# Two expert layers on one core: the low parts of a weight matrix in pieces of 1024 and 768 columns instead of 512 and 384

## The chip, the core and the metric

The kernel runs on one core of one Trainium2 chip. The metric is the device time of one execution in microseconds (us); the median of several runs is compared. TensorE multiplies matrices into the PSUM banks, VectorE and ScalarE work element by element, GpSimd does gathers, scatters and small arithmetic, and SyncE issues most transfers. Each engine works through its own queue in order and waits for others by semaphores.

## What is computed

The input is 14336 rows of 192 numbers. A causal convolution of 7 taps, one set of taps for each of 8 heads, comes first; the taps are a softmax. Then two layers of 8 experts follow, each expert with weights `w1` (192 x 1024) and `w2` (1024 x 192). Cut to what matters:

```python
x = conv(x, softmax(weight))
keep = x @ w_skip > 0                       # first layer: only these rows
e = argmax(x @ w_gate); g = softmax(...)[e]
x[keep] += g * (relu(x @ w1[e]) @ w2[e])
e = argmax(x @ w_gate2 + bias[modality])    # second layer: all rows
out = g * (relu(x @ w1[e]) @ w2[e])
```

## The kernel before

Products are made in half precision, with each number split into a high and a low part: high is the number, scaled by a power of two, rounded to 16 bits; low is the rounded rest. A product then takes three or five matmuls in place of one. So every weight matrix has to be *prepared* before it is used: loaded as 32-bit numbers, its power of two found, its high part rounded by ScalarE, and its low part formed by VectorE.

The work goes in three stages, which overlap. The first (to about 178 us) makes the convolution and the gate scores for 128 tiles of 112 rows, in 8 groups of 16 tiles, and the tables that say which row goes to which expert. The second (about 136 to 475 us) takes the first layer in blocks of 128 rows that belong to one expert. The third takes the second layer, mostly in pairs of blocks.

A block of the second stage is: 40 matmuls of 128 columns with `w1b` (the prepared `w1`) into two PSUM halves; for each half ScalarE writes `hh`, the high part after the relu, and VectorE `hlo`, the low part; and 24 matmuls of 192 columns with `w2b` on `hh` and `hlo` of the block before. VectorE then adds the residual into `x2a` or `x2s`. Two PSUM banks, later three, take turns for the halves, so TensorE can run a half or two ahead of `hlo`, not more.

The preparations are written as a generator, `prep`. It is run in two lanes beside the blocks: lane 0 prepares the eight experts of the first layer right into the buffers `w1b` and `w2b` that the blocks read, and lane 1 prepares four experts of the second layer into the buffers `o1` and `o2` (in the trace both are `o`). Both also store the result to memory (`s1a`, `s2a`, `s1b`, `s2b`; function `keep`, lines 409 and 411). Twelve preparations run in all; four more stand in a loop at the end that is entered only where the routing needs it.

What sets the order: `yield p` hands control back, and `prep` goes on `p` ticks later. There are four ticks in a block; p is 8 beside the blocks of the second stage (two blocks), 14 in the first stage, and 8 in lane 1. On TensorE, VectorE, ScalarE and GpSimd the instructions stand in the order in which the program writes them. On SyncE the compiler's scheduler places them.

One preparation, lines 368 to 392: `wt` holds the first 128 rows of `w1`, `wr` its other 64 rows (loaded in two transfers of 64 partitions), `w2t` all of `w2`. They lie in the buffers `ws1` (three slots) and `ws2` (one slot), both `ws` in the trace. The scales are in `sc` (`wsc` in the trace). Every low part is one VectorE instruction of the same form,

```python
nc.vector.scalar_tensor_tensor(out, v, scale, high, ALU.mult, ALU.subtract)
```

so it reads the 32-bit weights and the high part, both in SBUF, and writes 16 bits. The loads of the next expert are issued in between: `loadt` (line 308), `loadr` (line 315) once `wt` has been read, and `load2` (line 320) once `w2t` has been read.

Nearly all instructions of the trace carry line 71, that of the helper that records them; they are told apart by the names of their tiles.

Of the kernel before, what the change touches and what calls it, by code (L numbers as in the profile page):

```python
# [11 lines left out]
AF = mybir.ActivationFunctionType  # L12
ALU = mybir.AluOpType
# [4 lines left out]
D = 192  # L18
E = 8
F = 1024  # L20
# [95 lines left out]
class Moe:  # L116
# [179 lines left out]
    def prep(self, ws, pool, pq, dst, guard, done, es, lane, lag, pace, free, busy, first, early, side):  # L296
        nc = self.nc
        g = self.gram[lane].rearrange("p (i c) -> p i c", i=2)
        sq = g[:, 0, 0:2]

        def which(k, e):
            if k == 0:
                return slice(e, e + 1)
            return bass.ds(nc.sync.value_load(self.sel[0:1, e:e + 1], min_val=0, max_val=7), 1)

        def loadt(k, e):
            wt = pool.tile([128, F], F32, name="ws1", bufs=3)
            nc.sync.dma_start(wt, ws[k][0][which(k, e), 0:128, :].rearrange("a p f -> (a p) f"))
            return wt

        def loadr(k, e):
            wr = pool.tile([128, F], F32, name="ws1", bufs=3)
            x = which(k, e)
            for hf in range(2):
                nc.sync.dma_start(wr[hf * 64:hf * 64 + 64, :], ws[k][0][x, 128:192, :].rearrange("a p f -> (a p) f"))
            return wr

        def load2(k, e):
            w2t = pool.tile([128, 8 * D], F32, name="ws2", bufs=1)
            nc.sync.dma_start(w2t, ws[k][1][which(k, e)].rearrange("a p f -> (a p) f"))  # L320
            return w2t

        nxt = (loadt(*es[0]), loadr(*es[0])), load2(*es[0])
        yield first
        for n, (q, e) in enumerate(es):
            (wt, wr), w2t = nxt
            if early() and n < 2:
                for i, vs in enumerate(((wt,) * 8 + (wr[0:64],) * 8, (w2t,) * 12)):
                    for k, v in enumerate(vs):
                        c = k % 8 if i == 0 else k  # L330
                        v = v.bitcast(BF16)[:, c * 256 + 1:c * 256 + 256:2]
                        nc.tensor.matmul(g[:, i, :], v, v, start=(k == 0), stop=(k == len(vs) - 1))
                    yield 1
                yield 2
                dg = pq.tile([128, 512], F32, name="dg", bufs=1)[:, 0:256].rearrange("p (i c) -> p i c", i=2)
                nc.vector.tensor_tensor(dg, g, self.identf.unsqueeze(1).to_broadcast([128, 2, 128]), ALU.mult)
                ssq = pq.tile([128, 2], F32, name="ssq")
                nc.vector.tensor_reduce(ssq, dg, AX.X, ALU.add)
                yield 3
                nc.tensor.matmul(sq, self.ones, ssq, start=True, stop=True)  # L340
            else:
                sa = pq.tile([128, 4], F32, name="sa", bufs=2)
                for k, v in ((0, wt), (2, wr), (1, w2t[:, 0:4 * D]), (3, w2t[:, 4 * D:])):
                    jk = pq.tile([128, 512], F32, name="dg", bufs=1).bitcast(BF16)[:, 0:v.shape[1]]
                    nc.scalar.activation(jk, v, AF.Square, accum_out=sa[:, k:k + 1])
                    yield 2 if k < 3 else 5
                nc.tensor.matmul(sq, self.ones, sa[:, 0:2], start=True, stop=False)
                nc.tensor.matmul(sq, self.ones, sa[:, 2:4], start=False, stop=True)
            yield 2
            sc = pq.tile([128, 2], F32, name="wsc")  # L350
            self.pow2(sq, sc)
            nc.vector.tensor_scalar(sc, sc, 2.0 ** 30, 2.0 ** FT, ALU.min, ALU.mult)
            yield 1 if early() else 3
            while not guard(q, e) or busy[0]:
                yield 1
            busy[0] = True
            o1, o2 = dst(q, e)
            o2v = o2[:, :W2C].rearrange("p (c j) -> p c j", c=8)
            w2v = w2t.rearrange("p (c j) -> p c j", c=8)
            kf = pq.tile([128, 1], F32, name="kf")  # L360
            nc.vector.scalar_tensor_tensor(kf, sc[:, 0:1], 2.0, sc[:, 1:2], ALU.mult, ALU.mult)
            nc.vector.tensor_scalar(o2[:, W2C:].bitcast(I32), kf.bitcast(I32), EXPM, EXPM, ALU.bitwise_and, ALU.bitwise_xor)
            last = n + 1 == len(es)
            p = pace()
            if not last:
                nwt = loadt(*es[n + 1])
            h = F // 2
            lo = lambda o, v, s, i: nc.vector.scalar_tensor_tensor(o, v, s, i, ALU.mult, ALU.subtract)
            nc.scalar.activation(o1[:, 0, :], wt, AF.Copy, scale=sc[:, 0:1])
            yield p  # L370
            nc.scalar.activation(o2v[:, 0:4, 0:D], w2v[:, 0:4], AF.Copy, scale=sc[:, 1:2])
            lo(o1[:, 1, 0:h], wt[:, 0:h], sc[:, 0:1], o1[:, 0, 0:h])
            yield p
            lo(o1[:, 1, h:], wt[:, h:], sc[:, 0:1], o1[:, 0, h:])
            yield p
            nc.scalar.activation(o2v[:, 4:8, 0:D], w2v[:, 4:8], AF.Copy, scale=sc[:, 1:2])
            lo(o2v[:, 0:2, D:], w2v[:, 0:2], sc[:, 1:2], o2v[:, 0:2, 0:D])
            yield p
            lo(o2v[:, 2:4, D:], w2v[:, 2:4], sc[:, 1:2], o2v[:, 2:4, 0:D])
            if not last:  # L380
                nxt = (nwt, loadr(*es[n + 1]))
            yield p
            lo(o2v[:, 4:6, D:], w2v[:, 4:6], sc[:, 1:2], o2v[:, 4:6, 0:D])
            yield p
            nc.scalar.activation(o1[:, 2, :], wr, AF.Copy, scale=sc[:, 0:1])
            nc.vector.scalar_tensor_tensor(o2v[:, 6:8, D:], w2v[:, 6:8], sc[:, 1:2], o2v[:, 6:8, 0:D], ALU.mult, ALU.subtract)
            yield p
            nc.vector.scalar_tensor_tensor(o1[:, 3, 0:F // 2], wr[:, 0:F // 2], sc[:, 0:1], o1[:, 2, 0:F // 2], ALU.mult, ALU.subtract)
            if not last:
                nxt = nxt, load2(*es[n + 1])  # L390
            yield p
            nc.vector.scalar_tensor_tensor(o1[:, 3, F // 2:], wr[:, F // 2:], sc[:, 0:1], o1[:, 2, F // 2:], ALU.mult, ALU.subtract)
            done[q].add(e)
            busy[0] = False
            st = self.keep(ws, q, e, o1, o2, free)
            if early():
                for w in st:
                    yield w
                if not last:
                    yield max(1, lag() - 3 * (2 + q))  # L400
            else:
                side.add(st)
                if not last:
                    yield 4 + 12 * q
# [1178 lines left out]
```

## Time and profile before

| | before |
|---|---|
| median of three runs | 1002.71 us (1000.71 to 1004.94) |
| the profiled execution | 1001.22 us |
| its span, first to last instruction | 999.3 us |
| TensorE busy | 916.0 us (92%) |
| VectorE busy | 587.8 us (59%) |
| GpSimd busy | 513.7 us (51%) |
| ScalarE busy | 476.0 us (48%) |
| low parts of weights on VectorE | 96 instructions, 67.4 us together |

Times in the trace count from the span's start. "PE" is TensorE, "DVE" VectorE, "ACT" ScalarE, "POOL" GpSimd and "SP" SyncE. A duration in the trace runs from an instruction's start to its end, and consecutive VectorE instructions overlap a little, so the time that one takes from the queue is read from start to start. A busy TensorE is not TensorE at its peak: matmuls that follow one another more slowly still count as busy, so the number of matmuls in a stretch is read beside it.

### The profile page before, as it was taken

What the parts mean: (1) busy time and instruction counts of PE and PEld (TensorE: products, weight loads), DVE (VectorE), ACT (ScalarE), POOL (GpSimd) and SP (SyncE); (2) the same over time, 40 slices, a digit from 0 to 9 for tenths busy, and PEclk for the clock granted to TensorE, in tenths of its full rate; (3) what the DMA queues carried; (4) which work ended last, traced back from release to release, by engine and by line L of the source; (5) the groups of instructions that cost most, each with busy time, mean ns of one, the idle gap of its engine ahead of it and who ended that gap; (6) DMA issues with size and microseconds to landing.
All of it is one profiled execution on the core that took longest, in us unless ns stands there. A gap on an engine that the chain in (4) does not pass through costs nothing. (4 is left out here: it accounts for less than half of the span.)

```text
span 999.3 us, 28865 instructions
## 1 busy us (share of the span) xinstructions
PE 916.0 (92%) x11000; PEld 852.3 (85%) x11000; DVE 587.8 (59%) x1624; ACT 476.0 (48%) x895; POOL 513.7 (51%) x985
## 2 busy tenths in 40 slices
PE   6999868997999999976999999999989999999993
PEld 4666668987999999976888988999988999999992
DVE  5689977899798877543555465864332333333330
ACT  3877743545686654443645654333333333333430
POOL 4155543742646365562777675454544555555431
PEclk9999859999999999997999999999999999999997
DMA  9595576754868776599333333222492222332240
GB/s 318 192 334 187 186 198 191 197 137 132 237 181 249 214 223 197 163 233 329 91 95 98 109 98 111 70 64 62 135 295 63 73 74 69 74 73 74 74 122 16
DMA packets 106197, 150.79 MB, mean 151 GB/s; under 512 B 80591, under 2 KB 85689, under 8 KB 100800
## 3 DMA queue, kind: packets, MB, share of 16 engines
q1 hardware_dynamic: 91424, 119.34, 38.6%
q0 software_dynamic: 13920, 28.87, 12.1%
q8 instruction: 89, 1.46, 0.6%
q10 hardware_dynamic: 704, 0.63, 0.2%
q14 instruction: 60, 0.49, 0.2%
HBM read 174.22 MB, written 51.08 MB: 225 GB/s over the span
## 5 line engine op out<-in xcount | busy, mean ns | idle before, releaser
L71 PEld LDWEIGHTS <-w1b 128*128 128x128 f16 x4840 | 370.6, 99 | 43.1 <-issue 14.4
L71 DVE SCALAR_TENSOR_TENSOR ws<-bank,ws 128x512 f16<-128x512 f32 x220 | 151.3, 690 | 267.9 <-ACT ws L71 224.4
L71 PE MATMUL bank<-xp,w1b 128*128 128x256 f16 x2200 | 264.6, 274 | 5.2 <-DMA xp<-gt 2.9
L71 PE MATMUL bank<-w2b,ws 128*128 128x192 f16 x2640 | 239.2, 246 | 0.1
L71 PEld LDWEIGHTS <-ws 128*128 128x128 f16 (+2 forms) x2696 | 224.0, 98 | 2.7 <-issue 0.2
L71 POOL DMA_INDIRECT out_dram<-u,si x114 | 115.4, 1012 | 188.0 <-ACT u L71 76.0
L71 ACT ACTIVATE ws<-bank 128x512 f16<-128x512 f32 x220 | 130.6, 597 | 99.5 <-PE bank L71 89.0
L71 PE MATMUL bank<-xt,w1b 128*128 128x128 f16 x2640 | 165.6, 222 | 12.5 <-DVE hlo L71 7.4
L71 ACT ACTIVATE hh<-bank 128x512 f16<-128x512 f32 x132 | 78.5, 594 | 143.6 <-PE bank L71 133.0
L71 PE MATMUL bank<-w2b,hh 128*128 128x192 f16 x1056 | 141.2, 250 | 2.3 <-DMA w2b<-s2a 1.9
L71 PE MATMUL bank<-w2b,hlo 128*128 128x192 f16 x528 | 131.6, 249 | 0.6 <-DVE hlo L71 0.6
L71 ACT ACTIVATE u<-bank,c 128x192 f32<-128x192 f32 x114 | 48.1, 422 | 171.5 <-PE bank L71 148.0
L71 DVE SCALAR_TENSOR_TENSOR hlo<-bank,hh 128x512 f16<-128x512 f32 x132 | 90.0, 685 | 55.2 <-ACT hh L71 49.1
L71 PEld LDWEIGHTS <-hh 128*128 128x128 f16 x1056 | 96.3, 100 | 3.3 <-issue 2.9
L71 POOL DMA_INDIRECT gt<-rows,idxm x62 | 62.7, 1011 | 10.2 <-issue 6.9
L71 POOL TENSOR_TENSOR xs<-gt 128x128 f32<-128x128 f16 x124 | 53.7, 455 | 26.9 <-DVE x2a L71 13.0
L71 POOL DMA_INDIRECT gt<-rows,idx x58 | 57.5, 991 | 9.3 <-issue 6.7
L71 PE MATMUL bank<-xg,band 128*112 128x384 f32 x128 | 57.6, 537 | 1.7 <-DVE hl L71 1.7
L71 ACT COPY xtb<-bank 128x672 f16<-128x672 f16 x64 | 46.0, 720 | 19.2 <-PE bank L71 18.9
L71 PEld LDWEIGHTS <-hlo 128*128 128x128 f16 x528 | 52.4, 99 | 1.0 <-DVE hlo L71 0.8
L71 POOL DMA_INDIRECT gt<-rows,idxs x44 | 47.0, 1069 | 6.7 <-POOL c L71 3.3
L71 POOL TENSOR_SCALAR ef<-ef 128x4 f32<-128x4 f32 (+1 forms) x16 | 4.4, 277 | 86.8 <-DVE ef L71 86.8
(293 smaller groups left out, 1135.1 us busy)
## 6 DMA issues: line engine op xcount, KB each, us to landing
w1b<-s1b SPq DMA_DIRECT2D x59, 1024.0 KB
w2b<-s2b SPq DMA_DIRECT2D x59, 768.5 KB
xg<-in_x_dram SPq DMA_DIRECT2D x7, 1536.0 KB
rows<-hl SPq DMA_DIRECT2D x7, 1386.0 KB
ws<-in_moe_w_dram SPq DMA_DIRECT2D x12, 768.0 KB
s1a<-w1b SPq DMA_DIRECT2D x8, 1024.0 KB
w1b<-s1a SPq DMA_DIRECT2D x7, 1024.0 KB
s2a<-w2b SPq DMA_DIRECT2D x8, 768.5 KB
```

The lines of the kernel that those rows point to most:

```text
L71: r = f(*args, **kw)
```

## The change

In each preparation four pairs of VectorE instructions become four single ones. The low part of `wt` is formed in one piece of 1024 columns where the first piece of 512 stood; the low part of `w2t` in two pieces of 4 x 192 = 768 columns in place of four of 384; the low part of `wr` in one piece of 1024 columns, where the second of 512 stood. The sum of the waits stays 8 p. The load of the next `w2` is issued one step (p) earlier. ScalarE's part is the same.

```diff
-            h = F // 2
             lo = lambda o, v, s, i: nc.vector.scalar_tensor_tensor(o, v, s, i, ALU.mult, ALU.subtract)
             nc.scalar.activation(o1[:, 0, :], wt, AF.Copy, scale=sc[:, 0:1])
             yield p
             nc.scalar.activation(o2v[:, 0:4, 0:D], w2v[:, 0:4], AF.Copy, scale=sc[:, 1:2])
-            lo(o1[:, 1, 0:h], wt[:, 0:h], sc[:, 0:1], o1[:, 0, 0:h])
+            lo(o1[:, 1, :], wt, sc[:, 0:1], o1[:, 0, :])
+            yield 2 * p
+            nc.scalar.activation(o2v[:, 4:8, 0:D], w2v[:, 4:8], AF.Copy, scale=sc[:, 1:2])
+            lo(o2v[:, 0:4, D:], w2v[:, 0:4], sc[:, 1:2], o2v[:, 0:4, 0:D])
             yield p
-            lo(o1[:, 1, h:], wt[:, h:], sc[:, 0:1], o1[:, 0, h:])
-            yield p
-            nc.scalar.activation(o2v[:, 4:8, 0:D], w2v[:, 4:8], AF.Copy, scale=sc[:, 1:2])
-            lo(o2v[:, 0:2, D:], w2v[:, 0:2], sc[:, 1:2], o2v[:, 0:2, 0:D])
-            yield p
-            lo(o2v[:, 2:4, D:], w2v[:, 2:4], sc[:, 1:2], o2v[:, 2:4, 0:D])
             if not last:
                 nxt = (nwt, loadr(*es[n + 1]))
             yield p
-            lo(o2v[:, 4:6, D:], w2v[:, 4:6], sc[:, 1:2], o2v[:, 4:6, 0:D])
+            lo(o2v[:, 4:8, D:], w2v[:, 4:8], sc[:, 1:2], o2v[:, 4:8, 0:D])
             yield p
             nc.scalar.activation(o1[:, 2, :], wr, AF.Copy, scale=sc[:, 0:1])
-            nc.vector.scalar_tensor_tensor(o2v[:, 6:8, D:], w2v[:, 6:8], sc[:, 1:2], o2v[:, 6:8, 0:D], ALU.mult, ALU.subtract)
-            yield p
-            nc.vector.scalar_tensor_tensor(o1[:, 3, 0:F // 2], wr[:, 0:F // 2], sc[:, 0:1], o1[:, 2, 0:F // 2], ALU.mult, ALU.subtract)
             if not last:
                 nxt = nxt, load2(*es[n + 1])
-            yield p
-            nc.vector.scalar_tensor_tensor(o1[:, 3, F // 2:], wr[:, F // 2:], sc[:, 0:1], o1[:, 2, F // 2:], ALU.mult, ALU.subtract)
+            yield 2 * p
+            lo(o1[:, 3, :], wr, sc[:, 0:1], o1[:, 2, :])
```

The order of instructions on TensorE, ScalarE and GpSimd is the same before and after. VectorE's queue in the first preparation of lane 1, near 239 us of the trace, stands so before (the names with `o_` are the low parts, `oa` and `ob` belong to the routing tables, `hlo` to the blocks):

```order
L71 SCALAR_TENSOR_TENSOR o_2517<-ws_3331,wsc,o_2517 128x2x192
L71 SCALAR_TENSOR_TENSOR x2a<-bank_64,c,xs 128x192
L71 TENSOR_TENSOR oa<-iq,q 128x1024
L71 SCALAR_TENSOR_TENSOR o_2517<-ws_3331,wsc,o_2517 128x2x192
L71 SCALAR_TENSOR_TENSOR hlo<-bank_59,hh 128x512
L71 SCALAR_TENSOR_TENSOR o_2516<-ws_3319,wsc,o_2516 128x512
L71 SCALAR_TENSOR_TENSOR hlo<-bank_63,hh 128x512
L71 TENSOR_TENSOR ob<-iq,sl 128x496
L71 SCALAR_TENSOR_TENSOR o_2516<-ws_3319,wsc,o_2516 128x512
```

The same place of VectorE's queue afterwards:

```order
L71 SCALAR_TENSOR_TENSOR o_2505<-ws_3315,wsc,o_2505 128x4x192
L71 SCALAR_TENSOR_TENSOR x2a<-bank_64,c,xs 128x192
L71 TENSOR_TENSOR oa<-iq,q 128x1024
L71 SCALAR_TENSOR_TENSOR hlo<-bank_59,hh 128x512
L71 SCALAR_TENSOR_TENSOR hlo<-bank_63,hh 128x512
L71 TENSOR_TENSOR ob<-iq,sl 128x496
L71 SCALAR_TENSOR_TENSOR o_2504<-ws_3303,wsc,o_2504 128x1024
```

The last piece of `w2` has moved up into the one before it, and the first half of `wr` has moved behind the two `hlo`, into the piece that follows them.

SyncE's queue in the same preparation, near 232 us, stands so before (`ws` are the loads of the next expert, `xt` the transposes of the blocks' rows, `s1b` and `s2b` the stores of what was prepared):

```order
L1031 DMA_TRANSPOSE xt<-gt 128x3x128
L315 ISA
L315 DMA ws_4079<-in_moe_w_dram 64x1024
L315 ISA
L315 DMA ws_4079<-in_moe_w_dram 64x1024
L1031 DMA_TRANSPOSE xt<-gt 128x3x128
L320 ISA
L320 DMA ws_4171<-in_moe_w_dram 128x1536
L411 DMA s2b<-o_2517 128x1537
L409 DMA s1b<-o_2516 128x4096
```

The same place of SyncE's queue afterwards, with line numbers that are lower by 7:

```order
L315 ISA
L315 DMA ws_4061<-in_moe_w_dram 64x1024
L315 ISA
L315 DMA ws_4061<-in_moe_w_dram 64x1024
L1024 DMA_TRANSPOSE xt<-gt 128x3x128 x2
L320 ISA
L320 DMA ws_4121<-in_moe_w_dram 128x1536
L404 DMA s2b<-o_2505 128x1537
L402 DMA s1b<-o_2504 128x4096
```

The load of `wr` has moved ahead of a transpose; elsewhere in the queue a transpose, a load or a store changes places with a neighbour in the same way.

## Rows read from the trace of the kernel before

**Rows 1.** The page: busy us, share of the span and instructions of each engine.
```profile
PE 916.0 (92%) x11000; PEld 852.3 (85%) x11000; DVE 587.8 (59%) x1624; ACT 476.0 (48%) x895; POOL 513.7 (51%) x985
```

**Rows 2.** Two stretches: start:end, us, busy us (instructions) of each engine, clock, DMA.
```profile
278.00:301.00 23.00, 23.00 (x333) 23.00 (x330) 22.63 (x47) 17.58 (x33) 11.66 (x23) 1.00 0.69 208
363.00:425.00 62.00, 62.00 (x940) 62.00 (x938) 38.55 (x83) 30.30 (x58) 31.85 (x84) 1.00 0.56 161
```

**Rows 3.** TensorE's waits: 211 to 257 us (whole span: the same); 134 to 190.
```profile
PE bank L71 <- DVE hlo L71: 8.0, 5, 3.9
...
PE bank L71 <- DVE cuma L71: 7.8, 2, 4.9
```

**Rows 4.** The windows of the preparations, columns as in rows 2 (VectorE's third).
```profile
43.90:60.70 16.80, 14.27 (x172) 9.94 (x171) 15.34 (x51) 15.23 (x27) 4.70 (x11) 1.00 0.80 272
85.80:106.40 20.60, 17.28 (x200) 13.13 (x197) 19.79 (x63) 14.81 (x26) 13.55 (x27) 1.00 0.48 138
134.50:145.10 10.60, 4.79 (x46) 4.42 (x46) 10.35 (x32) 4.93 (x9) 4.13 (x10) 0.66 0.58 153
177.20:187.80 10.60, 10.60 (x160) 10.60 (x158) 10.37 (x17) 6.04 (x10) 10.10 (x22) 1.00 0.68 154
229.30:255.10 25.80, 20.07 (x269) 19.44 (x267) 25.35 (x63) 12.34 (x23) 10.12 (x22) 0.93 0.65 178
277.80:299.80 22.00, 22.00 (x317) 22.00 (x315) 21.63 (x46) 17.48 (x33) 10.48 (x21) 1.00 0.67 200
312.50:323.00 10.50, 10.50 (x158) 10.50 (x156) 9.58 (x18) 9.67 (x20) 7.76 (x15) 1.00 0.70 149
336.50:346.60 10.10, 10.10 (x146) 10.10 (x144) 9.77 (x21) 5.96 (x11) 4.23 (x9) 1.00 0.71 207
348.00:359.20 11.20, 11.20 (x160) 11.20 (x158) 10.61 (x22) 6.12 (x11) 6.68 (x14) 1.00 1.01 305
```

**Rows 5.** Pieces of lane 0: duration ns min/median/max, first and last start us.
```profile
L71 DVE SCALAR_TENSOR_TENSOR w1b<-ws,wsc,w1b x32: 719/743/1014, 44.0 to 358.4; 128x512 f16<-128x512 f32 x32
L71 DVE SCALAR_TENSOR_TENSOR w2b<-ws,wsc,w2b x32: 526/610/910, 48.2 to 356.0; 128x384 f16<-128x384 f32 x32
```

**Rows 6.** VectorE in order of time: start us, us, operation.
```profile
46.02 0.74 DVE L71 SCALAR_TENSOR_TENSOR w1b<-ws,wsc,w1b 128x512 f16<-128x512 f32 x1
46.68 0.61 DVE L71 SCALAR_TENSOR_TENSOR hl<-bank,s,hl 112x384 f16<-112x384 f32 x1
```

**Rows 7.** VectorE in order of time, a reduction over 768 columns.
```profile
234.22 0.94 DVE L71 TENSOR_REDUCE mx<-x2a 128x4 f32<-128x768 f32 x1
235.09 0.68 DVE L71 SCALAR_TENSOR_TENSOR hlo<-bank,hh 128x512 f16<-128x512 f32 x1
```

**Rows 8.** VectorE's pieces and GpSimd's additions, in order of time on each.
```profile
88.30 0.98 DVE L71 SCALAR_TENSOR_TENSOR w1b<-ws,wsc,w1b 128x512 f16<-128x512 f32 x1
...
312.51 0.91 DVE L71 SCALAR_TENSOR_TENSOR w1b<-ws,wsc,w1b 128x512 f16<-128x512 f32 x1
...
357.38 0.79 DVE L71 SCALAR_TENSOR_TENSOR w1b<-ws,wsc,w1b 128x512 f16<-128x512 f32 x1
...
312.33 1.25 POOL L71 TENSOR_TENSOR xs<-gt 128x128 f32<-128x128 f16 x2
...
433.37 0.69 POOL L71 TENSOR_TENSOR xs<-gt 128x128 f32<-128x128 f16 x2
```

**Rows 9.** VectorE, then TensorE, near 241 us [idle before <- what ended it].
```profile
241.14 0.68 DVE L71 SCALAR_TENSOR_TENSOR hlo<-bank,hh 128x512 f16<-128x512 f32 x1
241.74 0.80 DVE L71 SCALAR_TENSOR_TENSOR o<-ws,wsc,o 128x512 f16<-128x512 f32 x1
...
241.87 1.39 PE L71 MATMUL bank<-xt,w1b 128*128 128x128 f16 x20 [3.93 <-DVE hlo L71]
```

**Rows 10.** SyncE's own waits: us in total, times, longest us.
```profile
SPq L320 <- DVE w2b L71: 14.7, 5, 6.4
```

**Rows 11.** VectorE's waits: us in total, times, longest us.
```profile
DVE x2s L71 <- POOL c L71: 10.6, 11, 2.2
```

## The prediction

> **What bounds the kernel now.** I read the page's engine table first: TensorE is busy 92% of the span and VectorE 59%, which says only that VectorE cannot be the bound everywhere [rows 1]. The change touches nothing after some 393 us, so the question is what ends last while weights are being prepared. The table of stretches answers that. Between 363 and 425 us TensorE does 940 matmuls in 62.0 us, 66.0 ns each, with VectorE busy 38.55 us of it: that is TensorE at its own rate. Between 278 and 301 us it does 333 matmuls in 23.0 us, 69.1 ns each, with VectorE busy 22.63 us of 23.00. At 66.0 ns they would have taken 21.98 us, so about 1.0 us is lost there although "PE busy" reads 23.00 [rows 2]. The list of waits shows the same cause openly in two other places: between 211 and 257 us TensorE waits five times, 8.0 us together, for `hlo`, VectorE's second half of a PSUM eviction; between 134 and 190 us it waits twice, 7.8 us, for `cuma`, a routing table on VectorE [rows 3]. So VectorE sets the pace in parts of the preparation, and TensorE elsewhere. The table by preparation says where: VectorE's idle time is the window less its busy time, and in most of the nine windows it is under 0.6 us [rows 4].
>
> **What the change removes.** Each of the 12 preparations forms its low parts with 4 pieces of 512 columns and 4 of 384, and afterwards with 2 of 1024 and 2 of 768: 4 instructions fewer, 48 in all. The columns stay the same. So the gain is the part of an instruction that does not grow with its columns. The medians of 743 ns at 512 and 610 ns at 384 columns give 133 ns for 128 columns, 1.04 ns a column [rows 5]. A piece of 512 at 46.02 us lets the next instruction start at 46.68 us: 0.66 us from start to start, less 512 x 1.04 ns = 0.53 us, leaves **0.13 us** for each instruction [rows 6]. No row shows a piece of 1024 or 768 columns of this kind, so this is bounded. Below: the reduction over 768 columns at 234.22 us lets the next start at 235.09 us, 0.87 us, which leaves 0.87 - 0.80 = 0.07 us [rows 7]. Above: by its whole duration a piece has 743 - 532 = 211 ns that its columns don't explain [rows 5]. I take 0.13 us, because it comes from the same operation in the same queue; 48 x 0.13 = 6.2 us of VectorE time, 0.52 us for each preparation.
>
> [...]
>
> **What of it is on the path.** A preparation counts whole where VectorE's idle time in its window is below the 0.52 us that it saves, since then the queue behind it moves up and TensorE or the routing waits for that queue. It counts half where the idle time is larger, since part of the saving only widens an idle that is there [rows 4]:
> - 134.5 us (idle 0.25), 177.2 (0.23), 229.3 (two preparations, 0.45), 277.8 (two, 0.37) and 336.5 (0.33): 7 x 0.52 = 3.64 us. The pair at 277.8 brings 1.04 us, about the 1.0 us that TensorE loses there [rows 2].
> - 43.9 us (1.46), 85.8 (0.81), 312.5 (0.92), 348.0 (0.59): 4 x 0.26 = 1.04 us.
> - the twelfth, after 382 us, lies where VectorE is idle for over a third of the time and TensorE at its own rate [rows 2]: 0.
>
> Sum **4.7 us**; by the bounds 2.5 us (0.07) and 7.6 us (0.21).
>
> **What it moves.** The order on TensorE, ScalarE and GpSimd stays. On VectorE the second half of each pair goes where the first stood, except the last pair (`wr`), which goes where its second half stood. In the densest place this helps: before, `hlo` at 241.14 us, for which TensorE stood idle 3.93 us, has a piece of 384 right before it and a piece of 512 between it and the next `hlo` (0.72 us from 241.74 to that one's start, by the row's 0.80 less the overlap of 0.08 seen in rows 6); afterwards neither stands there [rows 6, 9]. The work comes later in the same full queue, so I count nothing beyond the sum. On the other side a piece in front of an `hlo` holds it 0.53 us longer (512 columns more) or 0.40 us (384 more); where VectorE is full that is only order, and elsewhere TensorE has no wait for `hlo` that it could lengthen [rows 3]. Taken at nothing; its price if that cover is gone is the rival below.
>
> SyncE's queue changes as well: the load of the next w2 is issued a step (8 ticks, two blocks) earlier, behind a last piece that is also a step earlier, and the load of the next `wr` finds its slot free earlier. SyncE stands 14.7 us in five waits at line 320 for w2 pieces [rows 10]; behind it stand transposes that are issued two blocks ahead of their use. Earlier loads are taken at nothing, up or down 1 us.
>
> Pieces that meet GpSimd are longer: 19 of the 96 exceed their median by over 30 ns, 3.1 us together, the first at 88.30 us (0.98 instead of 0.74), the last at 357.38 us (0.79) [rows 8]. Half as many starts can save up to half of it, 1.5 us, or nothing, since a longer piece meets more. I take 0 and keep both ends.
>
> The profiled execution took 1001.22 us, 999.3 of it the span, and lies 1.5 us under the median; 4.7 us off it gives 996.5. The median of the three runs, 1002.71, gives **998.0 us**, which I predict.
>
> **Rivals.**
> 1. *The saving is swallowed.* Only the places where a wait of TensorE for VectorE is written out pay: 134.5, 177.2 and 229.3 us, 4 x 0.52 = 2.1 us, so 1000.6. For it: all waits of TensorE for `hlo` lie before 257 us [rows 3]. Against: TensorE's lower rate at 278 us [rows 2].
> 2. *More is saved*: 0.21 us for each instruction and half the meetings with GpSimd, 7.6 + 1.5 = 9.1 us, so 993.6. For it: the durations of rows 5. Against: neighbouring instructions overlap by 0.08 us [rows 6].
> 3. *Long pieces hold `hlo` back, slower.* Place: the six preparations between 277 and 393 us and the two before 107 us, where TensorE or ScalarE has little to spare. Price: these eight have 16 + 16 long pieces, 16 x 0.53 + 16 x 0.40 = 14.9 us if every one stopped TensorE by its added length. It decides from a third of that on, 4.7 us; at two thirds, 9.9 - 4.7 = 5.2 us, so 1007.9. Against: all five waits for `hlo` lie between 211 and 257 us [rows 3], although pieces of 0.74 us stand before `hlo` in every preparation after that.
> 4. *GpSimd is held longer.* Two additions `xs` on GpSimd take 0.69 us at 433.37 us, with no piece near, and 1.25 us at 312.33 us, where a piece starts at 312.51 us and itself takes 0.91 us: each holds the other up [rows 8]. If a third of the 48 merges hold GpSimd by their added length (0.47 us in the mean), that is 7.4 us on GpSimd, and VectorE waits for its coefficient `c` 11 times, 10.6 us [rows 11]. If 2.5 us come through, the time is 1000.5. Against: what a long piece holds once, two short ones hold twice. [...]
> 5. *The change does not do what it says*: a piece of 1024 columns costs as much as two of 512. Then 1002.7; it is inside rival 1's bounds and has its chance with it.
>
> **How the numbers follow.** Forecast (gain of 3 to 6.5 us) 0.44, rivals 1 and 5 together 0.22, rival 2 0.15, rival 4 0.08, rival 3 0.11. A measurement of this kernel can tell about 0.5%, 5.0 us, from no change. Below 997.7 us lie rival 2 and half of the forecast: faster 0.37. Above 1007.7 us lies most of rival 3: slower 0.08. Within: 0.55. The range goes from rival 2's 993.5 to 1004.5, 1.8 us above no change for the small losses of rivals 3 and 4.
>
> **What would show it.** Right: pieces of 1024 columns near 1.27 us and of 768 near 1.01 us; VectorE busier by some 6 us less; the two waits for `cuma` 0.5 us shorter; the block after 363 us reached 4 to 5 us sooner. Wrong: the durations double (rival 5); new waits of TensorE for `hlo` outside 211 to 257 us (rival 3); GpSimd's `xs` longer and more waits for `c` (rival 4); stretches after 278 us at an unchanged 69 ns a matmul (rival 1).

## The result

The changed kernel took 1006.2 us (median of 11 runs, 1002.48 to 1011.2), the kernel before 999.42 us (11 runs on the same chip, 994.07 to 1004.94). The ratio is **1.0071, 95% interval 1.0049 to 1.0092**: some 7 us slower, where the prediction had a gain of 4.7 us. (A ratio here is the one on record; it differs from the quotient of the two medians printed beside it by up to 0.15%.) The profiled execution took 1002.48 us, its span 1000.6 us.

The page of the changed kernel, busy time and instructions of each engine, beside [rows 1]:

```profile
PE 916.4 (92%) x11000; PEld 852.6 (85%) x11000; DVE 581.1 (58%) x1576; ACT 475.4 (48%) x895; POOL 514.0 (51%) x985
```

VectorE has 48 instructions and 6.7 us less, as intended. Its pieces, by form (count | busy us, mean ns | idle before):

```profile
L71 DVE SCALAR_TENSOR_TENSOR w1b<-ws,wsc,w1b 128x1024 f16<-128x1024 f32 x16 | 21.4, 1339 | 0.6 <-ACT w1b L71 0.6
L71 DVE SCALAR_TENSOR_TENSOR w2b<-ws,wsc,w2b 128x768 f16<-128x768 f32 x16 | 16.7, 1045 | 0.0
L71 DVE SCALAR_TENSOR_TENSOR o<-ws,wsc,o 128x1024 f16<-128x1024 f32 x8 | 10.7, 1331 | 0.0
L71 DVE SCALAR_TENSOR_TENSOR o<-ws,wsc,o 128x768 f16<-128x768 f32 x8 | 8.1, 1009 | 0.0
```

They sum to 56.9 us, before 67.4. The waits of TensorE between 211 and 257 us, between 134 and 190 us, and between 257 and 430 us (us in total, times, longest); in the last stretch the kernel before has none:

```profile
PE bank L71 <- DVE hlo L71: 9.2, 7, 3.4
...
PE bank L71 <- DVE cuma L71: 7.5, 2, 5.0
...
PE bank L71 <- DMA xt<-gt: 3.2, 1, 3.2
```

The waits for VectorE hardly move against [rows 3]: those for `hlo` sum to 1.2 us more (in a second execution, below, to 7.8 us in five, 0.2 us less than before), those for `cuma` to 0.3 us less. The third line is new: TensorE waits for the transposed rows of a block. TensorE at that place, first in the kernel before, then in the changed one:

```profile
296.05 2.40 PE L71 MATMUL bank<-xt,w1b 128*128 128x128 f16 x40
300.26 1.28 PE L71 MATMUL bank<-xt,w1b 128*128 128x128 f16 x20
302.29 1.30 PE L71 MATMUL bank<-xt,w1b 128*128 128x128 f16 x20
305.82 2.40 PE L71 MATMUL bank<-xt,w1b 128*128 128x128 f16 x40
```

```profile
295.55 2.40 PE L71 MATMUL bank<-xt,w1b 128*128 128x128 f16 x40
303.08 1.28 PE L71 MATMUL bank<-xt,w1b 128*128 128x128 f16 x20 [3.15 <-DMA xt<-gt]
305.10 2.31 PE L71 MATMUL bank<-xt,w1b 128*128 128x128 f16 x20
311.51 2.40 PE L71 MATMUL bank<-xt,w1b 128*128 128x128 f16 x40
```

Up to 295.55 us the changed kernel is 0.5 us ahead; at its block of 311.51 us it is 5.7 us behind the same block before (305.82 us), and so are the blocks that follow (340.92 against 335.24 us). The first part of the loss is that wait, the second the clock. Stretches of the changed kernel, columns as in [rows 2] (granted clock third from the end):

```profile
303.00:305.00 2.00, 1.92 (x28) 1.92 (x28) 0.00 (x0) 0.60 (x1) 1.83 (x6) 0.83 0.97 408
305.00:307.50 2.50, 2.50 (x25) 2.50 (x23) 1.01 (x2) 0.05 (x1) 0.36 (x2) 0.50 1.02 358
307.50:311.00 3.50, 3.50 (x23) 3.34 (x23) 1.29 (x2) 0.55 (x1) 0.00 (x0) 0.50 0.61 164
311.00:315.00 4.00, 4.00 (x62) 3.98 (x61) 2.69 (x8) 1.65 (x3) 0.00 (x0) 0.98 0.56 222
```

After the idle time the granted clock of TensorE is 0.50 from 305 to 311 us; 20 matmuls take 2.31 us instead of 1.30.

Why `xt` was late stands in SyncE's queue (`SPq`; a row's duration is that of issuing the transfer, not of the transfer: the transpose issued at 293.89 us has 2.38 us there and lands at 299.04 us, as a table below shows). The kernel before:

```profile
291.93 1.21 SPq L315 DMA_DIRECT2D ws<-in_moe_w_dram  x2
293.19 0.58 SPq L411 DMA_DIRECT2D s2a<-w2b  x1
293.89 2.38 SPq L1031 DMA_TRANSPOSE xt<-gt  x1
297.68 0.36 SPq L320 DMA_DIRECT2D ws<-in_moe_w_dram  x1
298.15 1.65 SPq L1031 DMA_TRANSPOSE xt<-gt  x1
```

The changed kernel (its later line numbers are 7 lower):

```profile
289.92 1.32 SPq L315 DMA_DIRECT2D ws<-in_moe_w_dram  x2
295.89 0.36 SPq L320 DMA_DIRECT2D ws<-in_moe_w_dram  x1
296.35 2.49 SPq L1024 DMA_TRANSPOSE xt<-gt  x2
```

The load of the next `w2` (line 320, 768 KB) now stands ahead of the transpose. SyncE waits there for the last piece of `w2` on VectorE, which ends at 295.9 us, and the transpose is issued 2.5 us later than before (3.0 us later against the blocks, which are 0.5 us ahead) and behind those 768 KB. The kernel before has 768 KB ahead of that transpose too, the store of `s2a` (line 411), but SyncE issues both earlier.

### The profile page after: what moved, and what is told of

It reads as the page before. It is cut to its first block, busy times and chain, and to the rows that moved or that the text cites. A ratio compares the mean times of both kernels' runs of the same rounds, so it can differ in the third digit from the quotient of the medians.

```text
span 1000.6 us, 28807 instructions
## 1 busy us (share of the span) xinstructions
PE 916.4 (92%) x11000; PEld 852.6 (85%) x11000; DVE 581.1 (58%) x1576; ACT 475.4 (48%) x895; POOL 514.0 (51%) x985
```

## The experiments

Two theories. **Order** (S in the expectations): the earlier `load2` costs the time, through that one exchange on SyncE. **Length** (P): the longer pieces hold `hlo`, and so TensorE, back (rival 3). The first four kernels ran on one chip (before: 990.71 us, 35 runs).

**The changed kernel again.**

> The changed kernel itself once more, for a second profile and a ratio on the same chip as the three runs beside it. Two theories. S (SyncE's order): in the second preparation of lane 1 the load of the next w2 stands ahead of a block's transposes in SyncE's queue and waits there for the last w2 piece, so TensorE stands for a transpose near 300 us. P (piece length): pieces of 1.28 us hold the evictions hlo back. Both expect 1.005 to 1.009 of the kernel before. S expects again one wait of TensorE for xt of about 3 us near 300 us, and blocks 5 to 6 us late behind it; P expects the delay spread over several preparations.

998.32 us, ratio 1.0065 (1.0039 to 1.0091). The wait for `xt` is there again, 2.93 us.

**Long pieces, `load2` at its old step.**

```diff
             nc.scalar.activation(o1[:, 2, :], wr, AF.Copy, scale=sc[:, 0:1])
-            if not last:
-                nxt = nxt, load2(*es[n + 1])
-            yield 2 * p
+            yield p
+            if not last:
+                nxt = nxt, load2(*es[n + 1])
+            yield p
             lo(o1[:, 3, :], wr, sc[:, 0:1], o1[:, 2, :])
```

> All long pieces as in the changed kernel, but the load of the next w2 is issued where it was before (7 p instead of 6 p). In SyncE's queue it then stands behind a transpose in the second preparation of lane 1, as before; the loads of wr stay ahead of a transpose, as in the changed kernel. S expects no wait for xt near 300 us and 5 us less than the changed kernel: 0.997 to 1.002 of the kernel before. P expects no change against the changed kernel: 1.005 to 1.009.

991.29 us, ratio **1.0003** (0.998 to 1.0026). No wait for `xt` between 257 and 430 us. The loss is gone with all 48 merges in place; so is the gain.

**Short pieces, `load2` one step earlier** (the kernel before with only this):

```diff
+            if not last:
+                nxt = nxt, load2(*es[n + 1])
             yield p
             nc.vector.scalar_tensor_tensor(o1[:, 3, 0:F // 2], wr[:, 0:F // 2], ...)
-            if not last:
-                nxt = nxt, load2(*es[n + 1])
```

> All short pieces as before, but the load of the next w2 is issued one step earlier, right behind the last w2 piece. In SyncE's queue that puts it ahead of a transpose in the second preparation of lane 1, as in the changed kernel; nothing else in the queue moves. S expects a wait for xt near 300 us and 3 to 6 us more than before: 1.003 to 1.007. P expects 0.998 to 1.002.

994.9 us, ratio **1.0056** (1.0031 to 1.0082). In SyncE's queue of the whole program only one transfer changes its place: the load near 293 us now stands ahead of the transpose. SyncE, then TensorE:

```profile
292.47 0.58 SPq L411 DMA_DIRECT2D s2a<-w2b  x1
296.96 0.35 SPq L320 DMA_DIRECT2D ws<-in_moe_w_dram  x1
297.42 3.03 SPq L1031 DMA_TRANSPOSE xt<-gt  x2
```

```profile
295.33 2.40 PE L71 MATMUL bank<-xt,w1b 128*128 128x128 f16 x40
302.76 1.69 PE L71 MATMUL bank<-xt,w1b 128*128 128x128 f16 x20 [3.06 <-DMA xt<-gt]
305.19 2.07 PE L71 MATMUL bank<-xt,w1b 128*128 128x128 f16 x20
```

The same wait and the same slow matmuls, with the pieces untouched. Order holds, Length falls.

**Only the pieces of `w1` joined**, loads at their old steps.

> Only the w1 pieces are joined (24 of 1024 columns), the w2 pieces stay at 384 columns, and the load of the next w2 is issued where it was. In SyncE's queue that load stands behind a transpose as before; the loads of wr stand one transpose earlier, as in the changed kernel. S expects 0.996 to 1.001 of the kernel before (24 instructions fewer, 24 x 0.13 = 3.1 us of VectorE time, some of it on the path). P expects about half of the changed kernel's loss or more, 1.003 to 1.007, since these are the longest pieces.

990.32 us, ratio 0.9992 (0.997 to 1.0014).

What is it about the load that makes the transpose late: SyncE's waiting ahead of it, or the bytes? The next kernels ran beside 999.15 us (24 runs) of the kernel before.

**The load cut in two**, on the changed kernel: 192 columns (96 KB) ahead, the rest a step later.

```diff
-            nc.sync.dma_start(w2t, ws[k][1][which(k, e)]...)
+            nc.sync.dma_start(w2t[:, 0:D], ws[k][1][which(k, e), :, 0:D]...)
...
+        def rest(k, e, w2t):
+            nc.sync.dma_start(w2t[:, D:], ws[k][1][which(k, e), :, D:]...)
...
-            yield 2 * p
+            yield p
+            if not last:
+                rest(*es[n + 1], nxt[1])
+            yield p
```

> The changed kernel, but the load of the next w2 is cut in two: its first 192 of 1536 columns (96 KB) stay where the change put the load, ahead of the transpose near 293 us in SyncE's queue, and the other 1344 columns (672 KB) are issued one step later, behind that transpose. SyncE still waits there for the piece of w2 on VectorE, as long as in the changed kernel (to about 295.8 us); only the bytes ahead of the transpose shrink to an eighth. Two readings of the 5.5 us that the early load costs. Waiting: the transpose is late because SyncE stands still ahead of it, so the ratio to the kernel before stays near 1.0055 and TensorE waits for xt near 300 us for 3 us. Bytes: the transpose is late because 768 KB move ahead of it (3.7 us at the rates of the trace), so the ratio falls to 1.000 to 1.002 and the wait for xt near 300 us is gone or under 1 us. If both add up, the wait is in between, near 1 us, since the two make the transpose about 2.5 and 3.7 us later, and 3.1 us of the sum reach TensorE.

1001.3 us, ratio 1.0015 (0.9989 to 1.0041). SyncE, then TensorE:

```profile
293.32 1.52 SPq L315 DMA_DIRECT2D ws<-in_moe_w_dram  x2
299.28 0.36 SPq L320 DMA_DIRECT2D ws<-in_moe_w_dram  x1
299.75 1.20 SPq L1031 DMA_TRANSPOSE xt<-gt  x1
301.16 0.42 SPq L324 DMA_DIRECT2D ws<-in_moe_w_dram  x1
```

```profile
298.96 2.40 PE L71 MATMUL bank<-xt,w1b 128*128 128x128 f16 x40
304.10 1.28 PE L71 MATMUL bank<-xt,w1b 128*128 128x128 f16 x20 [0.76 <-DMA xt<-gt]
```

SyncE stands nearly as long as in the changed kernel (from 294.8 to 299.3 us, 4.4 us against 4.7), and the transpose is issued 0.8 us behind the first matmul of the block ahead, there as here (296.35 against 295.55 us); but TensorE waits 0.76 us instead of 3.15, and the 20 matmuls that follow at 306.13 us take 1.30 us, as before.

**Cut in the middle**: 384 KB ahead, 384 KB behind, run beside 999.17 us (17 runs).

> As the run before with the cut load, but the cut is in the middle: 768 of the 1536 columns of the next w2 (384 KB) stay ahead of the transpose near 293 us, the other half is issued one step later, behind it. With 96 KB ahead TensorE waited 0.76 us for xt near 304 us, with 768 KB 3.15 us. If the bytes ahead of the transpose set the loss, the wait is in proportion: 0.76 + 2.39 x 288 / 672 = 1.8 us, and the step from block 30 to block 31 lasts 6 to 7 us (before 4.1, with 96 KB 5.1, with 768 KB 8.9). If any load that waits for the piece of w2 has the same effect, the wait stays at 0.8 us; if only a whole load does, too. Ratio 1.002 to 1.005.

1003.84 us, ratio 1.0041 (1.0013 to 1.007). The transpose is again issued 0.8 us behind the block ahead (298.52 against 297.71 us):

```profile
303.79 1.28 PE L71 MATMUL bank<-xt,w1b 128*128 128x128 f16 x20 [1.71 <-DMA xt<-gt]
305.82 1.30 PE L71 MATMUL bank<-xt,w1b 128*128 128x128 f16 x20
```

1.8 us were expected. The 8.9 us in the expectation are the distance between the second halves of the two blocks, the 4.1 and 5.1 us that between their first halves; by first matmuls the step is 4.2 us before, 5.1 with 96 KB, 6.1 with 384 KB and 7.5 with 768 KB.

**As many bytes without a wait**: the kernel before and a copy from memory to memory, 768 KB, ordered behind the load of `wr`.

```diff
+            if lane and not last:
+                r = nc.sync.dma_start(self.junk[n], ws[q][1][e:e + 1]...)
+                self.tc.add_manual_dep(r.ins, mark[0].ins.name, ...)  # mark: the load of wr
             yield p
             nc.vector.scalar_tensor_tensor(o1[:, 3, 0:F // 2], wr[:, 0:F // 2], ...)
```

> The kernel before, with one transfer added in each of three preparations of lane 1: 768 KB from memory to memory, to a place that nobody reads, in SyncE's queue right behind the load of wr and, near 293 us, ahead of the transpose. It waits for nothing; the load of w2 stays behind the transpose. It is the complement of the cut load: there SyncE waits and few bytes are ahead, here as many bytes as the change puts ahead, and no wait. The transpose would be issued at 293.9 us as before, but land behind 768 KB, some 3.7 us later than it would alone. In the run with 96 KB, 4.4 us lay between the transpose's issue and the matmul that used it; in the kernel before 6.4 us, so it had 2.0 us to spare. If bytes and wait add up: TensorE waits about 1.7 us for xt near 300 us, ratio 1.001 to 1.003. If the bytes alone do it: a wait of 3 us and 1.005. If they do nothing without SyncE's wait: no wait near 300 us, and 1.000.

1006.97 us, ratio 1.0093 (1.0058 to 1.0128), with two more such copies in other preparations; a transpose near 308 us and a store near 360 us have moved by a place as well. SyncE, then TensorE:

```profile
293.77 0.56 SPq L390 DMA_DIRECT2D junk<-in_moe_w_dram  x1
294.44 2.82 SPq L1036 DMA_TRANSPOSE xt<-gt  x1
297.64 0.36 SPq L322 DMA_DIRECT2D ws<-in_moe_w_dram  x1
```

```profile
303.50 1.72 PE L71 MATMUL bank<-xt,w1b 128*128 128x128 f16 x20 [3.11 <-DMA xt<-gt]
305.95 2.05 PE L71 MATMUL bank<-xt,w1b 128*128 128x128 f16 x20
```

The transpose is issued almost when it was before (293.89 us), and TensorE waits 3.1 us for it all the same: bytes ahead of it are enough. This copy goes between two places in memory and the load into SBUF; no run shows whether the two delay a transpose alike, so the size is not to be compared to a tenth. Some of its further loss lies at the end of the second stage, where TensorE now waits 3.3 us for `w1b` from `s1a`, a wait that the kernel before has not; why, and where the rest lies, is not located.

The trace also keeps the semaphore events by which a transfer reports its landing. The table has all these kernels at the same blocks: A and B follow each other, D is two blocks behind B. "Issued" and "landed" are of the transpose that B uses (its last recorded event), "ahead" is the last transfer before it in SyncE's queue; the other columns are starts of first matmuls; all in us.

| kernel | ahead | A | issued | landed | B (wait for `xt`) | D | A to D |
|---|---|---|---|---|---|---|---|
| before | store, 768 KB | 296.05 | 293.89 | 299.04 | 300.26 (0) | 310.97 | 14.92 |
| long, `load2` late | loads of `wr` | 294.79 | 290.69 | 297.65 | 299.01 (0) | 309.72 | 14.93 |
| only `w1` long | store, 768 KB | 297.10 | 293.63 | 299.23 | 301.31 (0) | 312.01 | 14.91 |
| cut, 96 KB | load, 96 KB | 298.96 | 299.75 | 304.06 | 304.10 (0.76) | 314.81 | 15.85 |
| cut, 384 KB | load, 384 KB | 297.71 | 298.52 | 303.75 | 303.79 (1.71) | 314.48 | 16.77 |
| short, `load2` early | load, 768 KB | 295.33 | 297.42 | 302.72 | 302.76 (3.06) | 314.64 | 19.31 |
| changed, again | load, 768 KB | 299.53 | 300.32 | 306.79 | 306.84 (2.93) | 318.71 | 19.18 |
| changed | load, 768 KB | 295.55 | 296.35 | 303.03 | 303.08 (3.15) | 316.65 | 21.10 |
| copy | store and copy, 768 KB each | 296.01 | 294.44 | 303.46 | 303.50 (3.11) | 315.37 | 19.36 |

Wherever TensorE waits, B starts 0.04 or 0.05 us after the landing, so the transpose is what it waits for. In the kernel before, the store ahead landed at 298.90 us and the transpose at 299.04 us, 1.2 us before its use. Measured from A, the changed kernel issues it 3.0 us later, and from issue to landing it takes 6.7 us instead of 5.1: together 4.5 us, less the 1.2 us to spare, is the 3.3 us by which B is late. With short pieces it is 4.2 us of later issue and 0.2 us of longer way; with the copy, 0.6 us and 3.9 us. So later issue and more bytes ahead are each enough, and the change has both.

With the transpose issued 0.8 us behind A, and 96, 384 and 768 KB ahead, TensorE waits 0.76, 1.71 and 3.15 us: (3.15 - 0.76) / 672 KB is 3.6 us for 1000 KB. That holds for these three alone: behind the same 768 KB the transpose took 6.7 us from issue to landing in the changed kernel and 5.3 us with short pieces. The two loads of `wr` were still landing after its issue in the first (to 297.6 us) and not in the second (to 295.7 us); that this makes the difference is not shown.

A wait for `xt` of some 3 us is followed by 1.2 to 2.9 us more at a lower clock (0.50 in the changed kernel), one of 1.7 us by none. From A to D the changed kernel and that with short pieces lose 4.3 to 6.2 us, most of the measured 5.5 to 7.1 us, whose intervals reach down to 3.1 to 4.9; the cut in the middle loses 1.9 us there, of 4.1 (1.3 to 7.0). How the bytes ahead delay the transpose is not shown.

**The load in ScalarE's queue.** In lane 1, `load2` is issued by ScalarE at the same point, once with long pieces and once with short ones (before: 989.58 us, 22 runs).

```diff
-            nc.sync.dma_start(w2t, ws[k][1][which(k, e)]...)
+            q2, eng = (nc.scalar, nc.raw.scalar) if lane else (nc.sync, nc.sync)
+            q2.dma_start(w2t, ws[k][1][which(k, e, eng)]...)
```

> The changed kernel, but in lane 1 the load of the next w2 is issued from ScalarE, at the same point of the program, and so goes through ScalarE's DMA queue instead of SyncE's. SyncE no longer waits for the piece of w2 there, and the 768 KB move at about the same time as in the changed kernel, but not ahead of the transposes in their own queue. The scheduler moves some stores and loads on SyncE by a place or two. If the order within SyncE's queue is what makes the transpose late: TensorE has no wait for xt near 300 us, or under 0.8 us, and the ratio is back at 1.000 to 1.002. If the bytes in flight do it whatever their queue: a wait of 2 to 3 us and 1.004 to 1.007. [...]

992.5 us, ratio 1.0024 (0.9998 to 1.0051).

> The same move to ScalarE's queue with short pieces, against the run with short pieces and the load one step earlier in SyncE's queue (1.0056, a wait of 3.1 us for xt). Order within the queue: no wait for xt near 300 us, 1.000 to 1.002. Bytes in flight: a wait of 2 to 3 us, 1.004 to 1.006. Here the last piece of w2 on VectorE stands at the same step as the load, so ScalarE waits for it up to 1 us, ahead of one hh, in each of three preparations.

994.07 us, ratio 1.0055 (1.003 to 1.0081). In neither trace does TensorE wait for `xt` between 257 and 430 us: the transposes go ahead at 297.85 us (long) and 295.55 us (short). (The profiled execution with long pieces took 999.07 us, against a median of 992.5; its trace shows the order and the waits, not the loss.) But now ScalarE stands before the load. With short pieces, first ScalarE's and then TensorE's row:

```profile
299.66 0.60 ACT L71 ACTIVATE hh<-bank 128x512 f16<-128x512 f32 x1 [3.11 <-DVE o L71]
```

```profile
243.88 2.29 PE L71 MATMUL bank<-xt,w1b 128*128 128x128 f16 x20 [5.26 <-DVE hlo L71]
```

An `hh` waits 3.11 us behind the load (1.90 us with long pieces), and the wait of TensorE for `hlo` near 241.9 us grows from 3.93 us [rows 9] to 5.26. By block starts the run with short pieces loses 2.0 us between 187 and 335 us, of 5.4; the rest is not located. An issue took ScalarE 0.34 to 0.38 us. Since ScalarE waits, the load comes after the transposes (302.38 us long, 299.25 us short), so these runs do not tell whether bytes in another queue would delay them; that stays open.

**Only the pieces of `w2` joined.**

> Only the pieces of w2 are joined (2 of 768 columns in place of 4 of 384), those of w1 stay at 512; the loads stay at the places of the kernel before in the program. SyncE's queue keeps the transpose ahead of the load of w2 near 293 us; the scheduler puts that load ahead of a transpose in the next preparation, near 318 us, where the last piece of w2 ends at 319.4 us in the trace of before. If only the place near 293 us costs something: ratio 1.000, within 0.2%. If any load of w2 ahead of a transpose does: 1.002 to 1.005, with a wait of TensorE for xt after 320 us. If the longer pieces of w2 hold hlo back: a ratio over 1.002 with longer waits for hlo.

997.65 us (beside the 999.15 us above), ratio 0.9997 (0.9975 to 1.0019). The load ahead of a transpose near 318 us costs nothing: there is no wait for `xt`. That transpose is issued at 319.17 us and lands at 324.00 us, and no block near there is held up. Near 293 us, where the exchange costs a wait of 3 us, the transpose had 1.2 us to spare in the kernel before.

**Shorter pieces of `w1`**: the opposite of the change, 48 instructions more.

```diff
+            def lo4(o, v, s, i):
+                for x in (slice(0, h // 2), slice(h // 2, h)):
+                    lo(o[:, x], v[:, x], s, i[:, x])
-            lo(o1[:, 1, 0:h], wt[:, 0:h], sc[:, 0:1], o1[:, 0, 0:h])
+            lo4(o1[:, 1, 0:h], wt[:, 0:h], sc[:, 0:1], o1[:, 0, 0:h])
...
```

> The kernel before with every piece of w1 cut in two (256 columns): 48 instructions more, 48 x 0.13 = 6.2 us more VectorE time, the same as the change saves; in SyncE's queue the transposes near 293 us stay ahead of the load of w2. If the time of the pieces counts on the path as the prediction had it (three quarters of it): 4.7 us slower, 1.0047. If it counts for nothing, as the joined pieces suggest: 1.000, within 0.25%. VectorE's busy time should rise by 48 x 0.21 = 10 us by whole durations, its queue by 6.

1007.69 us (beside 999.15 us), ratio **1.0084** (1.0054 to 1.0114): neither number of the expectation. VectorE is busy 594.4 us, 6.6 more. TensorE's waits between 178 and 215 us of this kernel, then its stretch 188 to 200 us:

```profile
PE bank L71 <- DVE rC L71: 2.0, 1, 2.0
```

```profile
188.00:200.00 12.00, 9.99 (x123) 9.69 (x121) 9.28 (x20) 5.40 (x10) 9.03 (x16) 0.86 1.08 273
```

Before, that wait (for a routing table of VectorE) was 1.0 us, and the stretch held 168 matmuls at a clock of 1.00. By block starts this place costs 2.6 us, 1.0 of wait and 1.65 of clock. Another 1.0 us goes between 229 and 252 us and 0.5 us near 300 us: 4.1 us after 178 us. The other half of the loss is not located, since the first 178 us differ from run to run by as much (the changed kernel's block of 178.56 us started at 182.62 us in the other run).

## Why the prediction was wrong

**The step that failed** is SyncE's queue: "Earlier loads are taken at nothing, up or down 1 us", because transposes "are issued two blocks ahead of their use". They are written two blocks ahead; near 293 us SyncE reached one 6.4 us ahead of its use (293.89 to 300.26 us), and it landed only 1.2 us ahead of it. In the changed kernel it landed 4.5 us later against the blocks, 3.0 us of it by later issue and 1.5 us by a longer way, so that TensorE waited 3.15 us and then lost 2.9 us more at a lower clock (granted 0.50 from 305 to 311 us). The 14.7 us of [rows 10] are waits for `w2b`, the pieces of lane 0; the load near 293 us is lane 1's and waits for `o`, which is another line of the same list before:

```profile
SPq L320 <- DVE o L71: 10.2, 3, 5.9
```

I read how long SyncE stands there, not what is queued behind it at each of these waits. The rows of SyncE's queue that I looked at closely, near 232 us, belong to another preparation, where no load of `w2` passes a transpose.

**The size of the saving was right, its share on the path was not.** Pieces of 1024 and 768 columns take 1.33 to 1.34 and 1.01 to 1.05 us in the mean, 1.28 and 1.01 in the median (expected 1.27 and 1.01), VectorE is 6.7 us less busy (expected 6.2). But 4.7 us of it were to reach the end, and the long pieces alone give 1.0003 (all), 0.9992 (`w1`) and 0.9997 (`w2`); by the interval of the first they bring 2 us at most. Block by block, the kernel with long pieces and the late load is 0.77 us ahead of the kernel before at 178.88 us, 0.80 at 213.14, 1.29 at 241.87, 1.23 at 261.11 and 1.25 at 335.24 us: 0.5 us gained after 178 us, all of it between 229 and 256 us, where TensorE openly waits for `hlo`:

```profile
240.58 2.29 PE L71 MATMUL bank<-xt,w1b 128*128 128x128 f16 x20 [3.17 <-DVE hlo L71]
```

That wait was 3.93 us before [rows 9]. In the preparation pair at 277.8 us, which was to bring 1.04 us, the blocks keep their distances to 0.02 us. So the rule that a preparation counts whole where VectorE's idle time is below the saving [rows 4] was the mis-sized term, and the support taken from [rows 2] was no support: with the same block distances the row now reads

```profile
278.00:301.00 23.00, 23.00 (x327) 23.00 (x325) 22.08 (x41) 17.16 (x32) 12.98 (x26) 1.00 0.81 243
```

327 matmuls where 333 were, at no change of pace: the count of a stretch of 23 us is not good to the 5% that I read from it. Rival 1 (only written-out waits pay) was the right picture of this part, and still too large.

**The rivals.** Rival 3 forecast a slower kernel, by the wrong cause: the waits for `hlo` between 211 and 257 us sum to 7.5 us in five with long pieces and a late load, 8.0 in five before, and outside that stretch the changed kernel has no wait for `hlo` up to 430 us. Rival 4: VectorE's waits for `c` went from 10.6 us in 11 [rows 11] to 11.8 in 13, but between 257 and 430 us TensorE's only wait is that for `xt`, and GpSimd is 0.3 us busier in all. Rivals 2 and 5 are refuted by the totals and the durations. The slower side had its chance (0.08) from rival 3 alone; the mechanism that decided had no rival of its own, and the 1 us up or down for the earlier loads had no row behind it.

## What to carry to other kernels

Here a load that was issued one step earlier moved ahead of a transpose in its queue, and TensorE waited 3.15 us for that transpose. For a load that is to move, list, for each place, the transfer behind it, when that one is issued, when it lands and when it is used. An engine with hardly any idle time need not be on the path: VectorE was idle 0.37 us of 22.0 near 278 us [rows 4], and fewer instructions there left the blocks' distances as they were, to 0.02 us; its time counted where TensorE's wait for it is written out (0.5 us gained between 229 and 256 us). All the time saved brought a ratio of 1.0003, while the same time added lengthened such a wait from 1.0 to 2.0 us, and the clock there read 0.86 instead of 1.00. Separate the two halves of an edit (shorter work, moved issue) in the estimate, since each can be priced and run alone.

## What was not expected of the hardware

- A wait of TensorE of 2.9 to 3.15 us was followed by 20 matmuls in 2.05 to 2.31 us (1.30 before), and the granted clock read 0.50 from 305 to 311 us in the changed kernel; after waits of 0.76 and 1.71 us the same 20 took 1.30 us. Not every long wait does this: in the same changed kernel a wait of 3.44 us for `hlo`, ended at 241.46 us, left the clock at 1.00 up to 254 us.
- In the kernel before, the DMA transpose of 128 x 384 numbers near 293 us landed 0.14 us behind the store issued ahead of it in the same queue (299.04 and 298.90 us). In the three kernels that issue it 0.8 us behind A, TensorE's wait for it grew from 0.76 to 3.15 us with 96 to 768 KB of load ahead of it, 3.6 us for each 1000 KB.
- The fixed part of a VectorE piece came out alike in both directions: 6.7 us less of busy time for 48 instructions fewer and 6.6 us more for 48 more, 0.14 us each, against 0.13 us from start to start [rows 6].
